# Grouping the small matmuls of a delta-rule recurrence between the blocks of a feed-forward network

## The chip, the cores and the metric

The kernel runs on one core of a Trainium2 chip. The metric is device time in microseconds (us) of one execution; the time of a kernel is the median of several runs. The engines are called by their short names: PE (TensorE, matmuls), DVE (VectorE), ACT (ScalarE), POOL (GpSimd) and SP (SyncE, which here mostly issues transfers).

## What is computed

The reference is a delta-rule attention over 4 x 8 heads of 768 steps with 48 features, followed by a SwiGLU feed-forward network (FFN) over 3072 tokens. All values are float32.

```python
def _attn_ref(q, k, v, beta):
    k_n = k / (norm(k, axis=-1) + 1e-06)
    state = zeros((B, H, D, D))
    for t in range(S):
        kt, vt, bt = (k_n[:, :, t], v[:, :, t], beta[:, :, t, None])
        y[:, :, t] = einsum('bhd,bhde->bhe', q[:, :, t], state)
        v_old = einsum('bhde,bhd->bhe', state, kt)
        state = state + bt[..., None] * einsum('bhd,bhe->bhde', kt, vt - v_old)
    return y

def _moe_ref(x, w_gate, w_val, w_out):      # x: y as 3072 x 384
    g = x @ w_gate                          # 384 x 1536
    silu = g * (1.0 / (1.0 + exp(-g)))
    return silu * (x @ w_val) @ w_out       # 1536 x 384
```

## The kernel before

The sequence is cut into 12 chunks of 64 steps. For each chunk there is a **preparation** (transposes of k and q, their Gram products, and for each pair of chunks an inversion of a triangular system: `invert` on DVE, then `join` on PE), the **recurrence** (`advance`, four steps) and the **FFN** of the chunk's 256 tokens. Preparation and recurrence of the next chunk are placed between the FFN's matmuls of this one, at calls of `point`. What lies on PE between two FFN blocks is called a visit here. The small products use 64x64 or 32x32 parts of the PE array, the FFN all of it.

The recurrence, a generator whose steps end at `yield` (cut):

```python
def advance(c):
    ...
    if c > 0:
        scale_v(c)                              # DVE, on the v tile
    r = vin.pop(c)
    p_y = recur(ps_pair("p_y", "py"))           # PSUM, two banks
    if c > 0:
        p_r = recur(ps_pair("p_r", "px"))       # PSUM, two other banks
        for ... : nc.tensor.matmul(p_r..., kt[c]..., state...)   # 32 products
        for ... : nc.tensor.matmul(p_y..., qt[c]..., state...)   # 32 products
        nc.vector.tensor_tensor(out=r, in0=r, in1=p_r, op=ALU.subtract)
    yield
    p_u = recur(ps_pair("p_u", "px"))
    for ... : nc.tensor.matmul(p_u..., zt..., r...)
    uu = ...; nc.scalar.copy(uu..., p_u...)
    ...
    yield
    if 0 < c < NCH - 1:
        of_state()                              # p_s = k^T uu; state += p_s
    p_of_u()                                    # p_y += P uu
    y = ...; nc.scalar.copy(y..., p_y...)       # three copies, six for c = 0
    yield
    ...                                         # p_f: six 128x128 transposes of y
    nc.scalar.copy(x_v..., p_f...)              # x of the FFN
    yield
```

The preparation's products, two visits for each chunk, and the join, two more for each pair:

```python
def products(k_c, q_c):
    if k_c is not None: turned(k_c, False)      # transpose of k (late chunks: on DVE)
    if q_c is not None: turned(q_c, True)
    yield
    if k_c is not None:
        gram(k_c, False, None, (copies, copies))
        if k_c % 2 == 1:
            fills.append((k_c // 2, invert(k_c // 2)))
    if q_c is not None:
        gram(q_c, True)                         # DVE then applies the mask
    yield

def join(g):
    p_j = ps_pair("p_j", "px")[:, 0]...         # 64 products of 32x32
    t2 = ...; nc.scalar.mul(t2, p_j, -1.0)
    yield
    p_j = ps_pair("p_j", "py")...               # 64 products of 32x32
    ...                                         # copies into zt: ACT and DVE
    yield
```

For the first two pairs another join is used, which begins with two copies on ACT into `d_o`:

```python
def join_late(g, c, tags):
    d_o = work.tile([128, M, R], FP32, name="d_o", tag="z1", bufs=1)
    for s in range(2):
        nc.scalar.copy(d_o[...], d_v[..., 1])
    ...
```

The FFN of a chunk: `gate_val` for each pair of 128 hidden columns (24 matmul instructions in the trace), then `output` or, from chunk 3 on, `output_fast`. Inversion steps are handed to DVE by `fill(n)`, n at a time.

```python
def gate_val(c, f, fill, within=None):
    for w_sb, name in ((wg_sb, "p_gate"), (wv_sb, "p_val")):
        ps[name] = ps_ffn([128, 2, TOK], name)  # one of four PSUM banks
        ... 6 matmuls of 128x128 by 128x256 ...
        if name == "p_gate":
            nc.scalar.activation(sil, ps[name], ACTF.Silu)
            fill(2)
    nc.vector.tensor_tensor(out=hs[c, f], in0=sil, in1=ps["p_val"], op=ALU.mult)
    ...                                         # from chunk 3, f >= 6: sums of h on DVE
    fill(3)

def point(c):
    mine = c < NCH and steps("advance", c) < 4 and may_advance(c)
    if mine and steps("advance", c) > 0:
        step("advance", advance, c)
    elif not prep_step(c - 1) and mine:
        step("advance", advance, c)

for c in range(2, NCH):
    for f in range(0, FT, 2):                   # six pairs
        point(c + 1)
        gate_val(c, f, fill)
    point(c + 1)
    if c >= FAST: output_fast(c, fill)          # two more calls of point(c + 1)
    else: ...
    finish(c + 1)
```

At the start, until about 150 us, DVE also converts the FFN's weights from 64 to 32 bits (`convert`), with one exponent step per piece on ACT.

## Time and profile before

| | |
|---|---|
| time, median of 3 runs | 738.92 us (737.95 to 738.99) |
| span of the profiled run | 737.5 us |
| PE busy | 697.5 us (95%) |
| DVE busy | 473.1 us (64%) |
| ACT busy | 154.7 us (21%) |
| one FFN pair on PE, undisturbed | 2.59 + 2.59 us |

The profile is of one execution. A page gives each engine's busy time, then the span in 40 slices of 18.4 us, where a digit is the busy share in tenths (9 is 90% or more) and PEclk the clock granted to PE in tenths of full speed. The chain of work that ended last is followed back from the end: each piece stands with its start, its duration, the engine, the tile and line, and the number of instructions. In a timeline a row also names, in brackets, how long the engine was idle before it and what released it. In a list of waits the columns are the total in us, how often, and the longest. Ends of matmuls are modelled, so rows of PE overlap a little; the starts are the firmer numbers. For one matmul call of the program the trace holds two instructions.

### The profile page before, as it was taken

The numbers are of one execution on the slowest core, as the hardware profiler recorded it, in microseconds if no ns is written. First come the engines' busy times: TensorE is split into PE (matmuls) and PEld (weight loads), VectorE is DVE, ScalarE is ACT, GpSimd is POOL, SyncE is SP. The second block draws the span as 40 slices with busy tenths as digits, with TensorE's granted clock in tenths as the row PEclk, the third lists the DMA queues.
The fourth block names the chain that finished last, engine by engine and source line by source line (L and its number), as shares of the span: only waits on it lengthen the run. The fifth ranks groups of instructions, "written<-read, shape, count | busy, mean of one in ns | idle before, by whom it ended". The sixth has DMA issues, their size and how long they took to land.

```text
span 737.5 us, 22478 instructions
## 1 busy us (share of the span) xinstructions
PE 697.5 (95%) x10132; PEld 604.7 (82%) x10132; DVE 473.1 (64%) x977; ACT 154.7 (21%) x287; POOL 66.9 (9%) x46
## 2 busy tenths in 40 slices
PE   4657899999999999999999999999999999999997
PEld 3546788866787788988988988988988988989987
DVE  5999988978498163678854678854578853313122
ACT  3455443302401112011012011012011012021010
POOL 7008100201200000030000030000030000000000
PEclk9556999999999999999999999999999999999999
DMA  6775444121231012331302231302210100100000
GB/s 141 164 227 166 124 108 129 36 41 24 56 45 24 22 24 45 43 67 15 53 3 45 36 70 20 53 3 39 46 29 12 32 3 3 23 3 0 22 1 21
DMA packets 130735, 37.18 MB, mean 50 GB/s; under 512 B 122864, under 2 KB 125936, under 8 KB 130640
## 3 DMA queue, kind: packets, MB, share of 16 engines
q1 hardware_dynamic: 127184, 34.01, 22.7%
q10 hardware_dynamic: 3072, 1.57, 1.0%
q8 instruction: 79, 1.29, 0.7%
q0 software_dynamic: 384, 0.17, 0.1%
q14 instruction: 16, 0.13, 0.1%
HBM read 31.01 MB, written 4.72 MB: 48 GB/s over the span
## 4 chain that ended last, share of the span: by engine, by line
PE 83%; DVE 14%; issue 1%; DMA 1%; ACT 0%; ACTq 0%; SPq 0%; DVEq 0%
PE p_gate L847 23%; PE p_val L847 23%; PE p_o L959 17%; PE p_o L876 6%; DVE tmp L510 3%; PE p_g L444 3%; DVE zb L516 3%; PE p_u L763 2%; PE p_r L742 1%; PE p_s L794 1%; PE p_y L782 1%; PE p_y L751 1%; DVE last_h L287 1%; PE p_t L432 1%; DVE h_f L862 1%
## 5 line engine op out<-in xcount | busy, mean ns | idle before, releaser
L847 PE MATMUL p_gate<-x_ffn,wg_sb 128*128 128x256 f32 x864 | 204.4, 387 | 1.5 <-ACT x_ffn L830 1.5
L847 PE MATMUL p_val<-x_ffn,wv_sb 128*128 128x256 f32 x864 | 198.5, 379 | 0.0
L847 PEld LDWEIGHTS p_val<-x_ffn,wv_sb 128*128 128x128 f32 x864 | 163.8, 190 | 22.3
L847 PEld LDWEIGHTS p_gate<-x_ffn,wg_sb 128*128 128x128 f32 x864 | 161.1, 191 | 24.2 <-ACT x_ffn L830 2.0
L862 DVE TENSOR_TENSOR h_f<-sil,p_val 128x512 f32<-128x512 f32 x71 | 48.6, 684 | 147.5 <-PE p_val L847 147.0
L856 ACT ACTIVATE sil<-p_gate 128x512 f32<-128x512 f32 x72 | 43.0, 598 | 276.9 <-PE p_gate L847 247.3
L655 POOL TENSOR_TENSOR n_b<-mb,half 128x32 f32<-128x32 f32 x5 | 43.0, 8607 | 408.6 <-DVE mb L480 368.2
L959 PE MATMUL p_o<-wo_sb,h_f 128*128 128x192 f32 x432 | 75.6, 328 | 0.1
L959 PEld LDWEIGHTS p_o<-wo_sb,h_f 128*128 128x128 f32 x432 | 70.3, 190 | 1.2 <-DVE o_sb L969 0.7
L510 DVE TENSOR_TENSOR tmp<-zb,mb 128x31 f32<-128x31 f32 (+15 forms) x186 | 63.3, 340 | 12.2 <-PE p_j L630 6.8
L516 DVE TENSOR_TENSOR zb<-zb,tmp 128x31 f32<-128x31 f32 (+15 forms) x186 | 63.7, 343 | 6.5 <-DVE tmp L510 0.2
L969 DVE TENSOR_TENSOR o_sb<-o_sb,p_o 128x192 f32<-128x192 f32 x45 | 15.8, 350 | 53.4 <-PE p_o L959 36.2
L876 PE MATMUL p_o<-wo_sb,h_f 128*128 128x384 f32 x136 | 45.7, 490 | 0.0
L876 PEld LDWEIGHTS p_o<-wo_sb,h_f 128*128 128x128 f32 x136 | 25.3, 190 | 16.5
L959 PE MATMUL p_o<-last_k,h_f 128*128 128x192 f32 x180 | 32.2, 326 | 0.0
L959 PEld LDWEIGHTS p_o<-last_k,h_f 128*128 128x128 f32 x180 | 29.7, 190 | 0.0
L917 DVE TENSOR_TENSOR h_f<-h_f,h_f 128x256 f32<-128x256 f32 x54 | 22.4, 424 | 8.0 <-PE p_o L959 7.1
L959 PE MATMUL p_o<-last_h,h_f 128*128 128x192 f32 x144 | 26.3, 326 | 0.0
L959 PEld LDWEIGHTS p_o<-last_h,h_f 128*128 128x128 f32 x144 | 23.9, 190 | 0.0
L254 ACT ACTIVATE last_h<-last_h,rebias 128x512 int32<-128x512 uint32 (+2 forms) x26 | 15.3, 616 | 30.5 <-DVE last_h L246 30.4
L763 PEld LDWEIGHTS p_u<-vin,zt 64*64 64x64 f32 x768 | 13.7, 141 | 6.9 <-issue 3.2
L763 PE MATMUL p_u<-vin,zt 64*64 64x48 f32 x768 | 15.7, 228 | 2.4 <-DVE vin L759 1.2
(180 smaller groups left out, 692.6 us busy)
## 6 DMA issues: line engine op xcount, KB each, us to landing
vin<-in_v_dram SPq DMA_DIRECT2D x96, 48.0 KB
kn<-in_k_dram SPq DMA_DIRECT2D x40, 96.0 KB
out_dram<-o_sb SPq DMA_DIRECT2D x36, 96.0 KB
zt<-in_moe_w_out_dram SPq DMA_DIRECT2D x6, 384.0 KB
staged<-in_moe_w_out_dram SPq DMA_DIRECT2D x6, 384.0 KB
qpad<-in_q_dram SPq DMA_DIRECT2D x36, 64.0 KB
wo_sb<-in_moe_w_gate_dram SPq DMA_DIRECT2D x4, 512.0 KB
wo_sb<-in_moe_w_val_dram SPq DMA_DIRECT2D x4, 512.0 KB
```

Source lines behind the costliest of these rows:

```text
L444: nc.tensor.matmul(p_v[par][half_of(b if of_q else b ^ par), bp, j], kt[c][half_of(par), bp, j, b], xt[half_of(par), bp, j, b],)
L510: nc.vector.tensor_tensor(out=t_v, in0=zb[:, 0 : j + 1, j : j + 1].to_broadcast([128, j + 1, m]), in1=mb[:, j : j + 1, j + 1 : R].to_broad ...
L516: nc.vector.tensor_tensor(out=zb[:, 0 : j + 1, j + 1 : R], in0=zb[:, 0 : j + 1, j + 1 : R], in1=t_v, op=ALU.add,)
L655: nc.gpsimd.tensor_tensor(out=n, in0=mb.rearrange("p j i -> p (j i)")[:, 0 : R * R : R + 1], in1=half, op=ALU.pow,)
L763: nc.tensor.matmul(p_u[half_of(b), par, bp, j], zt[half_of(b ^ par), par, bp, j], r[half_of(b ^ par), par, bp, j], start=first, stop=True, ...
L847: nc.tensor.matmul(ps[name][:, i], w_sb[:, t, (f + i) * 128 : (f + i + 1) * 128], xts[c][:, t], start=(t == 0), stop=(t == KT - 1),)
L856: nc.scalar.activation(sil, ps[name], ACTF.Silu)
L862: nc.vector.tensor_tensor(out=hs[c, f], in0=sil, in1=ps["p_val"], op=ALU.mult)
L876: nc.tensor.matmul(p_o, hs[c, f - f % 2][:, f % 2, bp * 128 : (bp + 1) * 128], wo_sb[:, f], start=(f == 0), stop=(f == FT - 1),)
L917: nc.vector.tensor_tensor(out=out, in0=a, in1=b, op=ALU.subtract)
L959: nc.tensor.matmul(p[x, part], a(f - f % 2)[:, f % 2], b(f), start=not begun and f == 0, stop=f == FH - 1, skip_group_check=True,)
L969: nc.vector.tensor_tensor(out=out, in0=a, in1=b, op=ALU.add)
```

## The change

From chunk 4 on (the code's `c > 3`, the fifth chunk), the preparation's products no longer have visits of their own but go into those of the recurrence, by a fixed plan of stages. `advance` hands its first step over after the subtraction, and the product `p_y` moves into the visit of `p_u`. The first product of `join` takes one of the FFN's PSUM banks, so that it can stand in one visit with `p_r`. Apart from this, three products whose result nobody reads (`keep_awake`) are put ahead of the first FFN block, where PE waits for copies, so that PE's clock is up when the FFN begins; the copies into `d_o` are made ahead of their use; and one of the last output stores is issued by ACT instead of SP. Core of the diff, with cuts marked by "...":

```diff
+    def odd_heads(g, c):
+        ...                       # the two copies into d_o, made once, early or late
+    def keep_awake(n):
+        p = ps_pair("p_w", "px")[:, 0]
+        x = knp[0].rearrange("p bp h d -> p (bp h d)")
+        for _ in range(n):
+            nc.tensor.matmul(p, ident, x[:, 0:512])
 ...
     def join(g):
-        p_j = ps_pair("p_j", "px")[:, 0]...
+        p_j = ps_ffn([128, 512], "p_j")...
 ...
     def advance(c):
         r = vin.pop(c)
-        p_y = recur(ps_pair("p_y", "py"))
         if c > 0:
             ...                   # p_r
+            nc.vector.tensor_tensor(out=r, in0=r, in1=p_r, op=ALU.subtract)
+        yield
+        p_y = recur(ps_pair("p_y", "py"))
+        if c > 0:
             ...                   # p_y
-            nc.vector.tensor_tensor(out=r, in0=r, in1=p_r, op=ALU.subtract)
-        yield
         p_u = recur(ps_pair("p_u", "px"))
 ...
         p_of_u()
+        if c == 0:
+            keep_awake(2)
         y = ...
 ...                               # the transposes p_f
+        if c == 0:
+            keep_awake(1)
         x_v = ...
 ...
     def store(c, bp, o_sb):
         for b in range(2):
-            (nc.scalar if c < FAST else nc.sync).dma_start(
+            last = c == NCH - 1 and b == 1
+            (nc.scalar if c < FAST or last else nc.sync).dma_start(
 ...
+    def merged(c):
+        at, k_c, q_c = stage_of.get(c, (0, None, None))
+        g = c // 2
+        if at == 0:
+            ...                   # transposes of k_c and q_c
+        elif at == 1:
+            if c % 2 == 0 and g not in inverted:
+                return
+            a_step()              # p_r and the subtraction
+            if q_c is not None:
+                gram(q_c, True, "py")
+            if c % 2 == 0:
+                j_step()          # first product of the join
+            elif k_c is None:
+                at = 2
+        elif at == 2:
+            if c % 2 == 0:
+                j_step()          # second product of the join
+            gram_k("px")
+        elif at < 6:
+            a_step()
+        stage_of[c] = (at + 1, k_c, q_c)
+
     def point(c):
+        if c > 3:
+            merged(c)
+            return
 ...
         converts(2)
+        odd_heads(0, 1)
         second_inverse.append(invert(1))
```

## The prediction

> **What bounds the kernel now.** I read the page first: busy time and the strip of slices.

> ```profile
> PE 697.5 (95%) x10132; PEld 604.7 (82%) x10132; DVE 473.1 (64%) x977; ACT 154.7 (21%) x287; POOL 66.9 (9%) x46
> PE   4657899999999999999999999999999999999997
> PEclk9556999999999999999999999999999999999999
> ```

> TensorE (PE) is busy 95% of the span. The gaps and the half clock lie in the first five slices (18.4 us each). So two regimes: a front of about 90 us, and a long stretch where only what occupies PE or leaves it empty counts.

> For the long stretch I took the chain of work that ended last. Start, duration in us, engine, tile, line, instructions:

> ```profile
> 272.62 2.59 PE p_val L847 x12
> 275.21 1.08 PE p_r L742 x64
> 276.29 0.93 PE p_y L751 x64
> 277.22 2.79 PE p_gate L847 x12
> 280.01 2.59 PE p_val L847 x12
> 282.60 1.08 PE p_u L763 x64
> 283.68 2.79 PE p_gate L847 x12
> ```

> A visit is what stands between two FFN blocks. The first group of small products costs 1.08, a second in the same visit 0.93; the next FFN block costs 2.79 instead of 2.59. So a visit costs 0.15 + 0.20 = 0.35 us beyond its products.

> Then the waits of PE from 240 us on: three in all, each an idle of about 1 us.

> ```profile
> PE p_g L444 <- DVE kt L422: 1.9, 2, 1.0
> PE p_g L444 <- DVE qt L422: 1.0, 1, 1.0
> ```

> The PE timeline around the first of them:

> ```profile
> 342.47 2.75 PE L847 MATMUL p_val<-x_ffn,wv_sb 128*128 128x256 f32 x12
> 346.17 1.16 PE L444 MATMUL p_g<-kt 64*64 64x64 f32 x64 [0.94 <-DVE kt L422]
> 347.38 1.16 PE L444 MATMUL p_g<-qt,kt 64*64 64x64 f32 x64
> ```

> In the chain the output follows at 348.55. From the modelled end of p_val (342.54 + 2.59 = 345.13) that is 3.42 us; the same visit without a wait takes 2.02 (at 305.57), so the stall is 1.40. It repeats at 456 (1.40) and, with q alone, at 567 (2.30 against 1.09: 1.21). Together 4.0 us. The chain names the cause: VectorE (DVE) is behind with substitution steps (L510, L516) and the sums of h, and the transposes of k and q (1.26 us each) queue behind them.

> For the front, two lines of the chain and two of the PE timeline:

> ```profile
> 89.44 0.97 DVE vin L759
> 90.45 1.15 PE p_u L763 x64
> ```

> ```profile
> 61.56 1.54 PE L827 MATMUL p_f<-ident,y 128*128 128x128 f32 x6 [2.07 <-ACT y L817]
> 64.04 4.46 PE L847 MATMUL p_gate<-x_ffn,wg_sb 128*128 128x256 f32 x12 [0.95 <-ACT x_ffn L830]
> ```

> The chain runs through DVE almost without a break from 59 to 90 us (weight conversion) and goes to PE only with p_u of chunk 1. The clock is 0.50 in 60 to 65 us and 1.00 from 70 us, by the table of stretches.

> [...] p_gate at 64.04 took 4.46 against 2.86 warm, so the rise fell inside it. [...] the trace has 572 ns as the median issue of an output store on SyncE.

> **Part 1: merged visits.** I counted small-tile visits for chunks 4 to 11 in the order of PE instructions, leaving out p_f, which uses the full array. An even chunk had six (gram, join, join, p_r + p_y, p_u, p_s + p_y) and has four: p_r + gram q + join; join + gram k; p_y + p_u; p_s + p_y. Odd chunks 5, 7 and 9 have four before and after: the two grams part, but gram q moves in with p_r. Chunk 11 goes from four to three. Saved: 4 x 2 + 1 = 9 visits, at 0.35 us 3.15. No product goes away. The joins use 32x32 tiles, so a change of mode remains inside their visits; I carry that as a doubt of up to 0.15 us for each of eight merges.

> **Part 2: where the grams stand.** For an odd chunk the transposes of k and q now come at the first point of the FFN loop, with DVE free of substitution: the new order has them right after the last o_sb additions. Gram q comes one FFN pair (5.2 us) later and gram k two. Two transposes are 2.5 us, so both waits should go: 4.0 us. For an even chunk I walked DVE's new order by durations of this trace, from the end of an output: 7 substitution steps of 0.8 (5.6), two transposes 2.5, nine more steps about 6, two h products 1.4, the zt transposes 5.9; done at about 21 us. PE reaches the visit at 4 x 5.18 = 20.7 and needs zt after p_r and gram q, at 22.7. Subtraction ends at about 26.5 and the mask at 27.8; the next visit, which needs their PSUM, begins at about 29.3. This fits with 1.5 us to spare.

> **Part 3: p_y behind p_r's subtraction.** A pure exchange between two visits, with the same number of groups. p_y now stands ahead of p_u and gives the subtraction 0.93 us more. At 90.45 p_u still waits for DVE, whose order to that point is unchanged in every instruction. PE arrives earlier and waits longer; it gains only p_u's entry, 1.08 - 0.93 = 0.15.

> **Part 4: unread products and d_o.** A 128x512 product is two instructions of twice p_gate's columns: 2 x 0.43 = 0.86 us warm, 1.73 cold. The first two take up to 3.45 us in a hole of 2.07, so p_f may come 1.4 us later; it and p_gate then run warm, worth about 0.7 + 1.6, and the third fills the second hole of 0.95. So p_gate ends perhaps 1 us earlier. The moved d_o copies remove 1.4 us of PE waits at 73 to 75 us. But at 79.88 gram q waits for ScalarE's zt copies, which follow an exponent step fed by DVE, and at 90.45 comes DVE's subtraction. I count nothing for this part.

> **Part 5: last store.** The second half of the last output block is issued by ScalarE beside SyncE's. That is one issue of 0.57 us, less some overhead: 0.5.

> Sum: 3.15 + 4.0 + 0.15 + 0.5 = 7.8. I take off 0.9 for the 32x32 doubt and for a wait not seen. 738.9 - 6.9 = 732.0.

> **Rivals.** (a) DVE becomes the new wait. Inversions now start later and the join comes at the fifth FFN pair: if DVE is 2 to 3 us slower than my walk, p_j or gram k waits in chunks 6, 8 and 10. For it: only 1.5 us spare, and the old lag of 2 us at 345. Against it: during the visits of an even chunk no substitution is left. It would give 2 to 6 us back: 734 to 738. (b) The unread products hurt: they push p_gate, the first h product then holds DVE's queue at 73.3, and DVE sets p_u. For it: p_val ended there only 0.3 us ahead. Against it: the 1.4 us of d_o and the earlier clock give more than the products take. It would cost 1 to 2 us: about 733.5. (c) The front does gain: if ScalarE's order and not DVE's work set it, 1 to 3 us more come off: 729 to 731. Against it: DVE has no wait between 48 and 90 us. (d) The visit's price goes with the groups, not the visits: then part 1 is nil, and 735. Against it: a second group costs 0.93 everywhere in the steady stretch.

> **Range and chances.** Parts 1 and 2 carry 7 of the 7.8 us. Full success of both with a little of (c) makes 730; half of either lost with some of (a) makes 735 to 736. So 729.8 to 735.5. A change of over 2% needs 14.8 us, about twice the sum of everything I can point to, so within 2% is nearly certain.

> **What would show it.** Right: no wait of p_g on kt or qt after 240 us; visits of two and three groups where only the first is 0.15 dear, and 2.79 only once after each; p_u of chunk 1 still at about 90.4 with a longer idle ahead of it; the trace's end 0.5 us closer to the last o_sb addition. Wrong: new idle of PE ahead of p_j, p_g or p_u; p_u of chunk 1 moved by over 1 us either way; a join that costs as much inside a visit as alone.

## The result, and the profile after

| | before | after |
|---|---|---|
| time, median | 738.73 us (737.95 to 738.99, 4 runs) | 744.57 us (744.25 to 746.72, 4 runs) |
| ratio after to before | | 1.0087, 95% interval 1.0066 to 1.0108 |
| span of the profiled run | 737.5 us | 745.0 us |

The change made the kernel 5.8 us slower; 732.0 had been predicted. The profiled run of after is the slowest of its four, 2.2 us above the other three.

The page of the kernel after begins as before, with hardly more work on PE:

```profile
PE 701.3 (94%) x10138; PEld 608.8 (82%) x10138; DVE 472.2 (63%) x977; ACT 154.7 (21%) x287; POOL 65.3 (9%) x46
```

PE is 3.8 us longer busy (its six more instructions are the unread products) and 3.7 us longer idle. The waits of PE from 240 us on (engine, what waited, for what; total in us, times, longest):

```profile
PE p_j L727 <- issue: 5.0, 3, 1.7
PE p_j L741 <- issue: 2.5, 1, 2.5
PE p_j L741 <- DVE p_sb L459: 0.3, 1, 0.3
```

The waits on the transposes of k and q are gone. In their place stands "issue": idle for which the profile shows no releaser. The PE timeline of the first merged visit (chunk 4):

```profile
256.40 1.15 PE L762 MATMUL p_r<-state,kt 64*64 64x48 f32 x64
257.37 1.13 PE L444 MATMUL p_g<-qt,kt 64*64 64x64 f32 x64
258.42 0.82 PE L727 MATMUL p_j<-zt,a_sb 32*32 32x32 f32 x73
260.84 0.82 PE L727 MATMUL p_j<-zt,a_sb 32*32 32x32 f32 x55 [1.59 <-issue]
261.59 4.30 PE L873 MATMUL p_gate<-x_ffn,wg_sb 128*128 128x256 f32 x12
```

The idle lies inside a group, after 73 of 128 matmul instructions, where the profile shows nothing that PE waits for. The FFN product behind it then takes 4.30 instead of 2.86. Why, the table of stretches shows (after the stretch and its length come the busy time of PE, of PE's weight loads, DVE, ACT and POOL, each with its number of instructions; the last three columns are the granted clock, the share of the DMA engines, and GB/s):

```profile
258.00:259.00 1.00, 1.00 (x103) 0.93 (x95) 0.96 (x2) 0.00 (x0) 0.00 (x0) 1.00 0.07 16
259.00:260.00 1.00, 0.24 (x29) 0.13 (x15) 1.00 (x2) 0.00 (x0) 0.00 (x0) 1.00 0.00 0
260.00:261.00 1.00, 0.16 (x19) 0.17 (x23) 0.90 (x2) 0.00 (x0) 0.00 (x0) 1.00 0.00 0
261.00:262.00 1.00, 1.00 (x56) 0.94 (x48) 1.00 (x2) 0.30 (x1) 0.00 (x0) 0.56 0.06 16
262.00:263.00 1.00, 1.00 (x3) 0.76 (x3) 1.00 (x2) 0.29 (x1) 0.00 (x0) 0.50 0.00 0
```

Behind the idle the clock is at 0.50. And two single transfers of 16 KB stand out (16 GB/s for 1 us), with nothing else moving. The page has a queue of such packets, one of two whose kind is "instruction" (packets, MB, share of the DMA engines):

```profile
q8 instruction: 79, 1.29, 0.7%
```

1.29 MB in 79 packets is 16.3 KB each. PE has 10,138 matmuls and 10,138 weight loads in this trace, 257 for each of the 79 packets, so I take this queue for PE's program, in blocks of about 128 matmuls with their weight loads. The pages of two later runs agree with it: e3 has 512 matmul instructions more than the kernel before and e8 has 640, and their queues have 4 and 5 packets more, one for every 128.

```profile
q8 instruction: 83, 1.36, 0.8%
q8 instruction: 84, 1.38, 0.8%
```

The trace also has the times of the single packets. The one seen above runs from 258.13 to 259.26; PE stops at 259.24 and resumes at 260.84, 1.6 us after the packet has ended. In after and in the runs e3, e7, e8, e10 and e12, which are described below, PE stops 26 times after 240 us with no releaser shown. The four stops of after end 1.58, 1.34, 1.46 and 1.45 us after the end of such a packet. In the traces of before and after no packet of q8 begins less than 3.36 us after the one before. A merged visit uses as many instructions as two packets come to on average, in 3.24 us where it runs through (chunk 8, 494.31 to 497.55); a visit before used at most as many as one packet.

Where the time went, by the distances between starts. In chunk 4 the join takes 3.17 us instead of 1.22 and p_gate 4.13 instead of 2.69: 3.4. Chunk 6: 1.9 at the join. Chunk 8: the second visit, 4.5. Chunk 10: 3.5. Together 13.3. The end of chunk 2's output comes 0.9 later (251.29 against 250.37). The spans differ by 7.5, and 0.3 is gained at the tail, so about 6.4 us must have been gained elsewhere: 13.3 + 0.9 - 6.4 - 0.3 = 7.5.

In the front, p_u of chunk 1 starts at 89.92 (90.45 before), released by DVE's subtraction as before, but PE had been idle longer, and what follows runs at half clock in this run (0.50 granted from 90.46 to 93.88):

```profile
89.92 1.56 PE L785 MATMUL p_u<-vin,zt 64*64 64x48 f32 x64 [1.67 <-DVE vin L770]
91.42 4.05 PE L873 MATMUL p_val<-x_ffn,wv_sb 128*128 128x256 f32 x12
```

### The profile page after: what moved, and what is told of

Same layout as the page of the kernel before. It is cut to its first block, busy times and chain, and to the rows that moved or that the text cites. A ratio compares the mean times of both kernels' runs of the same rounds, so it can differ in the third digit from the quotient of the medians.

```text
span 745.0 us, 22487 instructions
## 1 busy us (share of the span) xinstructions
PE 701.3 (94%) x10138; PEld 608.8 (82%) x10138; DVE 472.2 (63%) x977; ACT 154.7 (21%) x287; POOL 65.3 (9%) x46
## 3 DMA queue, kind: packets, MB, share of 16 engines
q10 hardware_dynamic: 3232, 1.77, 1.1%
q8 instruction: 79, 1.29, 0.7%
## 4 chain that ended last, share of the span: by engine, by line
PE 83%; DVE 13%; issue 3%; DMA 1%; ACT 0%; SPq 0%; ACTq 0%; DVEq 0%
PE p_gate L873 24%; PE p_val L873 23%; PE p_o L986 17%; PE p_o L902 6%; PE p_g L444 2%; DVE tmp L510 2%; DVE zb L516 2%; PE p_u L785 1%; PE p_s L816 1%; PE p_y L775 1%; PE p_y L804 1%; PE p_r L762 1%; PE p_f L851 1%; DVE last_h L287 1%; DMA kn<-in_k_dram 1%
## 5 line engine op out<-in xcount | busy, mean ns | idle before, releaser
L873 PE MATMUL p_gate<-x_ffn,wg_sb 128*128 128x256 f32 x864 | 206.6, 390 | 0.3 <-ACT x_ffn L856 0.2
L873 PEld LDWEIGHTS p_gate<-x_ffn,wg_sb 128*128 128x128 f32 x864 | 163.8, 194 | 24.4 <-ACT x_ffn L856 1.3
L510 DVE TENSOR_TENSOR tmp<-zb,mb 128x31 f32<-128x31 f32 (+15 forms) x186 | 63.3, 340 | 12.0 <-PE p_j L651 6.7
L516 DVE TENSOR_TENSOR zb<-zb,tmp 128x31 f32<-128x31 f32 (+15 forms) x186 | 63.7, 343 | 6.4
L254 ACT ACTIVATE last_h<-last_h,rebias 128x512 int32<-128x512 uint32 (+2 forms) x26 | 15.3, 616 | 36.5 <-DVE last_h L246 36.5
L796 ACT COPY uu<-p_u 128x768 f32<-128x768 f32 (+1 forms) x13 | 9.6, 748 | 40.4 <-PE p_u L785 40.4
```

Source lines behind the costliest of these rows:

```text
L254: nc.scalar.activation(power.bitcast(I32), power, ACTF.Relu, bias=rebias, scale=8.0)
L510: nc.vector.tensor_tensor(out=t_v, in0=zb[:, 0 : j + 1, j : j + 1].to_broadcast([128, j + 1, m]), in1=mb[:, j : j + 1, j + 1 : R].to_broad ...
L516: nc.vector.tensor_tensor(out=zb[:, 0 : j + 1, j + 1 : R], in0=zb[:, 0 : j + 1, j + 1 : R], in1=t_v, op=ALU.add,)
L873: nc.tensor.matmul(ps[name][:, i], w_sb[:, t, (f + i) * 128 : (f + i + 1) * 128], xts[c][:, t], start=(t == 0), stop=(t == KT - 1),)
```

## The experiments

**e1: the join in visits of its own.** In even chunks the plan of stages becomes:

```diff
+        elif c % 2 == 0:
+            if at == 1:  # p_r and gram q, not waiting for the inversion
+            if at == 2:  # gram k
+            if at == 3:  # first product of the join, once inverted
+            elif at == 4:  # second product
```

> The changed kernel, but in even chunks the two products of the join and gram k have visits of their own again (p_r + gram q; gram k; join; join; p_y + p_u; p_s + p_y); no visit holds more than 128 matmul instructions. Theory F (PE's instructions come in blocks of 256, and a visit of 512 drains what is at hand faster than the next block arrives): no idle without a releaser in or after a join and no half clock behind it; the changed kernel's losses there (12.6 us in its profile) go, 8 visits come back (+2.8), so about 735 us. Rival D (the merged visits wait for VectorE's copies, mask and zt transposes, which stand in nearly the same order here): idle at the join stays, above 740. Rival M (the change from 64x64 to 32x32 tiles inside one visit costs 1.6 us): also about 735; the doubled join tells M from F.

Measured: 744.39 us, 1.0071 (1.0047 to 1.0096). No "issue" is left at the joins, but the time did not fall. All that PE waits for after 240 us:

```profile
PE p_g L444 <- DVE qt L422: 6.9, 3, 2.7
```

My own placing was the fault: p_r with gram q now came at the second FFN pair, when DVE was still at its transposes. The PE timeline, first of the three:

```profile
363.75 1.15 PE L762 MATMUL p_r<-state,kt 64*64 64x48 f32 x64
367.56 1.99 PE L444 MATMUL p_g<-qt,kt 64*64 64x64 f32 x64 [2.66 <-DVE qt L422]
369.48 4.86 PE L873 MATMUL p_gate<-x_ffn,wg_sb 128*128 128x256 f32 x12
```

Here a hole with a plain cause, a wait of 2.66 us for DVE, is also followed by half clock (p_g 1.99 and p_gate 4.86). As a measure of the time, e1 settled nothing; as to the idle at the join, it went with the merging, as F and M say.

**e2: unread products ahead of the join.** Work is added to the changed kernel:

```diff
+        p_w = ps_ffn([128, 512], "p_j")
+        for _ in range(2):
+            nc.tensor.matmul(p_w, ident, wg_sb[:, 0, 0:512])
+        p_j = p_w.rearrange("p (c m i) -> p c m i", c=2, m=M)
```

> The changed kernel with two unread 128x512 products (4 matmul instructions, 1.73 us of PE) put between gram q and the join's first product, in the four merged visits of chunks 4, 6, 8 and 10. Theory F: the added time is time in which the next block of instructions arrives, so the idle of 1.6 to 1.7 us inside the join shrinks to near nothing, the half clock behind it goes in chunks 4 and 10, and the total changes by -3 to +2 us. Rivals D and M: the idle stays and the products add 4 x 1.73 = 6.9 us: about 751.

Measured: 740.67 us, 1.0025 (1.0018 to 1.0032): 3.9 us less than the changed kernel, with 6.9 us more work. PE has no wait at all after 240 us. The same visit:

```profile
256.72 1.99 PE L723 MATMUL p_j<-wg_sb,ident 128*128 128x512 f32 x4
258.63 1.29 PE L730 MATMUL p_j<-zt,a_sb 32*32 32x32 f32 x128
259.85 2.86 PE L876 MATMUL p_gate<-x_ffn,wg_sb 128*128 128x256 f32 x12
```

The join runs through and p_gate is warm (this profile is of the fastest of 20 runs, 739.50). The expectation gave D and M 751. D falls. M does not fall by this run, since the products also stand between the 64x64 and the 32x32 tiles; e10, e3 and e8 settle it.

**e7: the same products behind the join's first half**, as the control:

```diff
         # after the first product of the join
+        p_w = ps_ffn([128, 512], "p_w")
+        for _ in range(2):
+            nc.tensor.matmul(p_w, ident, wg_sb[:, 0, 0:512])
```

> The control to e2: the changed kernel with the same two unread 128x512 products in the same four visits, but behind the join's first product instead of ahead of it. Theory F: the products come too late to give the next block time, so the idle of 1.6 us inside the join stays; 744.6 + 6.9, less what of the half clock they take over: 748 to 752, at least 7 us above e2 (740.7). If the gain of e2 was only that the wide products keep the clock up, this should do it about as well: 740 to 744.

Measured: 750.31 us, 1.0149 (1.0132 to 1.0166), 9.6 us above e2 with the same work. The idle is where it was:

```profile
256.29 0.82 PE L727 MATMUL p_j<-zt,a_sb 32*32 32x32 f32 x73
258.70 0.67 PE L727 MATMUL p_j<-zt,a_sb 32*32 32x32 f32 x55 [1.59 <-issue]
259.31 3.68 PE L734 MATMUL p_w<-wg_sb,ident 128*128 128x512 f32 x4
```

It stops at the same instruction, the 73rd, as in the changed kernel. So the filler of e2 helps by giving time ahead of that instruction and not by keeping PE busy in general.

**e10: one unread product instead of two.**

```diff
-        for _ in range(2):
+        for _ in range(1):
```

> e2 with one unread product per visit (0.86 us) instead of two. Theory F: the idle inside the join shrinks by what is added, from 1.6 to about 0.8 us, and a shorter hole no longer brings the half clock: 744.6 - 2 to -5, so 739.5 to 743. If the filler acts in another way than by giving time (by its mere presence between the tile sizes), the idle is either unchanged at 1.6 or gone.

Measured: 741.69 us, 1.0047 (1.0038 to 1.0055).

```profile
256.05 1.13 PE L723 MATMUL p_j<-wg_sb,ident 128*128 128x512 f32 x2
257.10 0.80 PE L730 MATMUL p_j<-zt,a_sb 32*32 32x32 f32 x71
258.19 0.69 PE L730 MATMUL p_j<-zt,a_sb 32*32 32x32 f32 x57 [0.28 <-issue]
```

The product moves the join by 1.05 us (256.05 to 257.10), and the idle shrinks from 1.59 to 0.28 in chunk 4, from 1.73 to 0.33 in chunk 6, and from 1.71 to 0.65 in chunk 10: about by what was added. In chunk 8 the second visit still idles, 1.49. The idle answers to the dose; under M it would have been 1.6 or gone. (This profile is of the fastest of the eleven runs, 738.81.) The stop now comes after 71 instructions of the join instead of 73, with two more ahead of it. Counted from the start of the program it is the same place: in after, e3, e7 and e10 alike, PE stops in chunk 4 after 3,911 matmul instructions, as one would expect if a block ended there.

**e3: the kernel before, the join's first product issued twice.** No merging, no change of tile inside the visit; results are overwritten by equal ones.

```diff
-        for c in range(2):
+        for c in (0, 1, 0, 1):
```

> The kernel before, with the 64 products of the join's first half issued twice into the same place (256 matmul instructions in that visit instead of 128), nothing else changed; four visits. The second issue is extra work, 4 x about 1.05 = 4.2 us of PE. Theory F: each of these visits now drains the instructions at hand: idle of 1 to 2.5 us without a releaser inside it, some with the half clock behind: 738.7 + 4.2 + 6 to 13 = 749 to 756. Rivals D and M: nothing to wait for and no change of tile size inside the visit: 743.

Measured: 761.75 us, 1.0307 (1.0286 to 1.0328), above even F's range.

```profile
249.64 2.46 PE L706 MATMUL p_j<-zt,a_sb 32*32 32x32 f32 x231
254.32 0.39 PE L706 MATMUL p_j<-zt,a_sb 32*32 32x32 f32 x25 [2.23 <-issue]
254.64 4.54 PE L847 MATMUL p_gate<-x_ffn,wg_sb 128*128 128x256 f32 x12
```

All four visits stall, 8.7 us of idle in total. The p_gate behind the one shown takes 4.38 from start to start, at half clock. Together, the four joins take 15.3 us more than at 1.22 each, and the four p_gate 8.0 more than at 2.69 each. I had added 6 to 13 us for idle and clock, and they came to 8.7 and 8.0; the second issue, put at 4.2 in all, took 15.3 - 8.7 = 6.6. The direction is F's, the size was not.

**e8: the kernel before, the grams of k and q issued twice.** 256 matmul instructions in a visit, as in the merged one, but all of 64x64 tiles.

```diff
+        twice = c >= 5 if of_q else c >= 7
+        for _ in range(2 if twice and c < (10 if of_q else NCH) else 1):
             for bp, j, par, b, _ in every():
                 nc.tensor.matmul(p_v[par]..., kt[c]..., xt...)
```

> The kernel before with the grams of k and q issued twice in their common visit, five visits (k of chunks 7 to 11, q of 5 to 9): 256 matmul instructions per visit as in the changed kernel's merged visit, but all of 64x64 tiles, at 2 us per 128. Extra PE work 5 x 2.0 = 10 us. Theory F: a block of 256 instructions lasts 2.0 us here against about 3.2 us for the next to arrive, so each visit idles about 1 us without a releaser: 738.9 + 10 + 4 to 12 = 753 to 761. If the idle belongs to 32x32 tiles and not to the number of instructions: 749, no idle.

Measured: 755.56 us, 1.0221 (1.0199 to 1.0243): 16.7 us, 6.7 beyond the extra work, as F said. All that PE waits for after 240 us:

```profile
PE p_g L446 <- issue: 7.4, 5, 1.7
PE p_g L446 <- DVE kt L422: 1.9, 2, 0.9
PE p_g L446 <- DVE qt L422: 1.0, 1, 1.0
```

Five visits, five holes. So here the idle goes with the number of instructions in a row and not with 32x32 tiles.

**e4: the kernel before with the front alone** (the `keep_awake` and `odd_heads` of the change, nothing else).

> The kernel before with only the front of the change: the three unread products and the earlier d_o copies. My step: VectorE sets p_u of chunk 1 at about 90 us whatever PE does before, so 738.7 within 0.5. Rival H (PE arrives earlier at that wait, [...] p_u with the FFN product behind it runs at half clock): 739.5 to 740.5, with p_val after p_u at about 4 us instead of 2.8. Rival G (a real gain from the warm clock at the first gate): 736 to 737.5.

Measured: 739.56 us, 1.0014 (1.0005 to 1.0023): 0.65 us slower than before in the same round, a little over my 0.5 and at H's lower edge. In its profile p_u follows a wait of 1.22 us at full clock; but that run, at 738.80, is one of the fastest of twelve, so where the 0.65 lies is not shown and H is not ruled out. The warm gate of the front is real (p_gate takes 2.79, start to start, against 4.39) and brings nothing: in this profile PE then waits 2.2 us for ACT, the half clock comes behind that hole, and the next p_gate takes 4.95 instead of 3.14.

**e12: the changed kernel without the front** (the same two taken out).

> The changed kernel without its front (no unread products, d_o copies where they were). If the loss of 5.8 us lies in the merged visits alone: the same as the changed kernel, 744.6 within 0.7. If the front has a share of it (p_u and the product behind it at half clock in the changed kernel's profile, 1.6 us): 742.5 to 743.5.

Measured: 743.53 us, 1.0064 (1.0042 to 1.0086), single runs from 740.16 to 746.11. The waits inside the joins are there in this profile too (7.4 us in total), so most of the loss is there without the front. About 1 us of the 5.8 may be the front's; the spread leaves open whether it is anything.

**e5: e1 with p_r and gram q one FFN pair later.**

```diff
-                if g not in n_t:
+                held[c] = held.get(c, 0) + 1
+                if g not in n_t or held[c] < HOLD and g not in inverted:   # HOLD = 2
                     return
```

> The split version e1, with p_r + gram q of an even chunk one FFN pair later. In e1 no idle was left at the join, but gram q, now at the second FFN pair, waited 2.7, 2.7 and 1.5 us for VectorE's transpose of q, twice with half clock behind it: 11.7 us in its profile. If that is all that was wrong with e1, this takes 744.4 - 11.7 = 732.7, between 731.5 and 734.5: faster than both kernels. If theory F is wrong or incomplete and splitting the join only moves the loss, it stays above 738.

Measured: 737.94 us, 0.9985 (0.9974 to 0.9996). Better than before, but not by what I had worked out, because another DVE wait took the place of the last:

```profile
376.95 1.16 PE L444 MATMUL p_g<-kt 64*64 64x64 f32 x64 [1.77 <-DVE vin L770]
378.05 4.54 PE L873 MATMUL p_gate<-x_ffn,wg_sb 128*128 128x256 f32 x12
```

Gram k needs the PSUM that holds p_r until DVE has subtracted it, and DVE is behind with the transposes of zt.

**e6: e5 without the front.**

> e5 without the front of the change (no unread products, d_o copies where they were). The front alone cost the kernel before 0.65 us (739.56 against 738.91). If this adds up, 0.3 to 1 us below e5, about 732; if the front pays off together with the moved p_y, equal or above e5.

Measured: 738.11 us, 0.9982 (0.9975 to 0.9990), equal to e5.

**e9: e6 with the grams together and p_r after them, and gram k copied out by ACT instead of DVE.**

```diff
-                a_step()
+                if k_c is None:
+                    a_step()
+                else:
+                    gram(k_c, False, "px", (nc.scalar.copy,) * 2)
                 if q_c is not None:
                     gram(q_c, True, "py")
             if at == 2:
                 if k_c is None:
                     at = 3
                 else:
-                    gram_k("px")
+                    a_step()
```

> e6 (split join, no front) with another order in even chunks: gram k and gram q together at the third FFN pair, gram k copied out by ScalarE, then p_r alone. In e5 gram k had waited twice 1.77 us for VectorE's subtraction to give its PSUM free, once with half clock behind it, 5.5 us in its profile. If that wait is gone and none takes its place: 738 - 5.5 = 732.5, between 731.5 and 734.5, with no wait of PE over 0.3 us after 240 us. If VectorE's lag shows up at another product (p_r, or the join for zt): 735 to 739.

Measured: 732.94 us, 0.9928 (0.9915 to 0.9942): faster than both kernels, as worked out. PE has no wait after 240 us. The order and the engine of the copies changed together; which of the two was needed is not shown. Its page:

```profile
PE 696.3 (95%) x10132; PEld 605.5 (83%) x10132; DVE 469.5 (64%) x973; ACT 156.4 (21%) x291; POOL 64.6 (9%) x46
```

**e11: e9 with the front put back.**

> e9 with the front of the change put back (three unread products, earlier d_o copies). If VectorE sets p_u of chunk 1 at about 90 us whatever PE does before it, the same as e9: 732.9 within 0.5. If the warm clock at the first gate pays: 731 to 732. If the longer hole ahead of p_u brings the half clock: 733.5 to 734.5.

Measured: 733.33 us, 0.9924 (0.9910 to 0.9937): the same as e9. p_u starts at 90.25 after a wait of 1.67 us, here at full clock.

## Why the prediction was wrong

The step that failed is part 1, "Saved: 4 x 2 + 1 = 9 visits, at 0.35 us 3.15." It took a visit's price from rows of visits with at most 128 matmul instructions, and applied it to visits of 256. It left out that a row of 256 might not run as two rows of 128 do. In before and after the packets of q8 begin 3.36 us apart or more, and 128 small matmuls are used up in 2.1 us in e8 (at 304.64) and, by the row above of 231 in 2.46, in about 1.4 in e3. From the point 128 matmuls ahead of a stop to the resumption it is 3.3 us (chunk 4), 3.3 (6) and 3.6 (10) in after, and by estimate from the rows 3.6 in e8 (resuming at 310.07) and 3.6 in e3 (at 254.32). That a block is asked for at that point is not shown. That the idle depends on the number of instructions in a row and on the time given is shown by e2, e7, e10, e3 and e8. That a missing block is the cause remains an inference: the four stops of after end 1.3 to 1.6 us after the end of a packet.

None of my rivals held this. (a) looked for a new wait at the right products (p_j, chunks 4 to 10) and of about the right size, but of DVE; in the changed kernel DVE's part is 0.3 us. The view that could have warned me was in the profile before: PE idle with the releaser "issue", 10.6 us in 0 to 60 us at p_m, p_g and p_j, all runs of small products.

The size was off as well. The join takes 1.22 us as the third group of a visit just as alone, and gram k behind a join 1.10 against 1.09 alone: here going to another small tile was not cheaper than coming from the full array. So a merged join saves only the 0.20 on the way out. From the starts, chunks 6 and 8 save 0.38 each, 4 and 10 save 0.55, chunk 11 0.35: 2.2 us and not 3.15. Of the doubts listed, this one was right: a join costs as much inside a visit as alone.

Point by point, the rest. Part 2 was right in the changed kernel: no wait on kt or qt, and my walk of DVE gave the join and gram k their place (the one DVE wait is 0.27, on the mask in chunk 8). In e1 and e5, with p_r and gram q at the second and third FFN pair of chunk 6 instead of the fifth, a gram waits up to 2.7 or 1.8 us. Part 3 held: p_u is released by DVE at 89.92, with the longer idle ahead of it. Part 4 held as "nothing": e11 equals e9, and e4 loses 0.65. That half clock may come behind PE's longer hole ahead of p_u was in neither part; the changed kernel's profile shows it (a hole of 1.67 us, then about 1.6 us lost at p_u and p_val), five later profiles with a hole of 1.65 to 1.7 (e2, e5, e6, e11, e12) do not. Part 5 was too high: from the last o_sb addition to the end of the span it is 3.41 us against 3.67, so 0.26.

Taken together: 4.0 (part 2) + 2.2 (part 1 as it is) = 6.2, close to the 6.4 us left over as gained above, and the 0.9 I had taken off for the doubt and a wait not seen stood against 13.3.

What stays open. In chunk 8 the first merged visit ran through, and the second, of 192 matmul instructions, stopped for 2.49 us. Its packet began only at 504.36, 6.9 us after the one before; from there to the resumption it is 2.6 us, as at the other three stops of after (2.5 to 2.8). What makes a block be asked for is not shown. For the clock the traces of before and after show more: the changes of the granted clock lie 3.41 us or whole multiples of it apart there. In after, the holes of chunks 4, 8 and 10 lie with 1.59, 2.41 and 1.71 us inside one such stretch, and the next ran at 0.50; the hole of chunk 6 (386.43 to 388.17) is cut by the point at 387.42 into 0.99 and 0.75, and the clock stayed. No rule follows from this: in e11 the hole of 1.67 us ahead of p_u had the clock at 1.00 behind it (90 to 94 us).

## What to carry to other kernels

Count instructions, not only microseconds, where small matmuls are gathered: here, from chunk 4 on, a run of up to 128 small matmuls with their weight loads never stopped PE without a releaser, and runs of 256 did so in 16 of 17 cases (after, e12, e3, e8), for up to 2.3 us; of 192, two of four did (2.5 us in after, 1.4 in e12). Gather small products between large ones only up to the first number, unless a run shows that more costs nothing. Where idle with no releaser stands inside a group, repeat instructions or add time ahead of it, as e3 and e2 did, before looking for a missing buffer. What did pay was where a product stands against the engine that feeds and empties it: e9 differs from e6 in the order of the products within the visits and in the engine that copies gram k out, and 4 to 5 us lie between them.

## What the runs showed of the hardware that was not expected

Adding about 6.9 us of unread work made the changed kernel 3.9 us faster (e2); the same work one group later made it 5.7 us slower than the changed kernel (e7). In chunk 4 of the changed kernel a hole of 1.59 us on PE was followed by a clock of 0.50 in the next 3.41 us, after 167 us at 1.00. It was not so each time: behind the hole of 1.73 us in chunk 6 the clock stayed at 1.00.
